# Reordering the first key matmuls of a gated linear-attention / token-MLP kernel, with smaller first copies

## The chip, the cores and the metric

The kernel runs on one core of one Trainium2 chip. The metric is the device time of an execution in microseconds (us). Executions come in a fast and in a slow state (lower granted TensorE clock); comparisons below use fast runs. A ratio is the mean time of one kernel's fast runs over the mean time of the other's of the same rounds, so it is not quite the ratio of the medians that are quoted. A profile is one execution recorded by the hardware profiler; its span runs from the first to the last instruction and is about 1.7 us shorter than the execution's time.

## The reference

Input `x` is 2048 tokens of 512 features, bf16. Two blocks are mixed by a gate per token.

```python
def _A_ref(x, wqkv, wo):                 # linear attention, 32 heads of 16
    q, k, v = ...                        # x @ wqkv, split in heads
    phi = lambda t: jnp.where(t > 0, t + 1, jnp.exp(t)) + 1e-6
    pq, pk = phi(q), phi(k)
    kv = einsum("bhsd,bhse->bhde", pk, v);  z = einsum("bhsd->bhd", pk)
    o = (pq @ kv) / (pq . z + 1e-6)
    return o @ wo
def _B_ref(x, w1, b1, w2, b2):           # MLP over tokens
    h = layernorm(x)
    u = gelu(einsum("bsd,sf->bdf", h, w1) + b1)
    return (einsum("bdf,fs->bds", u, w2) + b2).transpose
g = sigmoid((x * gate_w).sum(-1))
return g * A(x) + (1 - g) * B(x)
```

Only the first step matters here: keys `k = x @ wk` for 16 tiles of 128 tokens, followed by `phi`.

## The kernel before

The program writes the order of instructions of each engine by hand. A key matmul needs `x` transposed (features on the partitions). For most tiles a transposing DMA makes that; it is too late for the first three tiles (the first such DMA landed at 6.94 us in the profile below), so TensorE transposes those (four 128x128 matmuls with the identity), and VectorE and ScalarE copy the result from PSUM to SBUF.

```python
    # loads, in this order (x tiles are 128 KB, halves of the key weights 256 KB)
    load_x(nc.sync, 0, 1)
    load_wk(nc.scalar, 0, 2)      # chunks 0 and 1 of the key weights
    load_x(nc.sync, 1, 1)
    load_wk(nc.scalar, 2, 2)      # chunks 2 and 3
    load_x(nc.sync, 2, 1)
    # ... transposing loads of tiles 3 to 15, further weights ...
    warm_up(6)                    # six 512-column matmuls on constants

    def transpose_tile(t):
        pt = bank("pt")           # one PSUM bank of the eight
        for k in range(ND):       # ND = 4 chunks of 128 features
            mm(pt[:, k * P : (k + 1) * P], xs[:, t, k * P : (k + 1) * P], ident[:], True, True)
        H = ND // 2
        src = pt[:].rearrange("p (k s) -> p k s", k=ND)
        dst = xT[:, :, t * P : (t + 1) * P]
        nc.vector.tensor_copy(out=dst[:, 0:H], in_=src[:, 0:H])
        nc.scalar.activation(out=dst[:, H:], in_=src[:, H:], func=ACT.Copy)

    def k_part(t, ks):            # key matmuls of tile t for feature chunks ks
        if t not in kaccs:
            kaccs[t] = bank("kacc")
        for k in ks:
            mm(kaccs[t][:], xT[:, k, t * P : (t + 1) * P], wk_sb[:, k, :], k == 0, k == ND - 1)

    HEADS = 3
    transpose_tile(0)
    transpose_tile(1)
    for t in range(2):
        k_part(t, range(2))
    transpose_tile(2)
    ln_step(0)
    for t in range(HEADS):
        k_part(t, range(2 if t < 2 else 0, ND))
        k_phi(t)
    ln_step(1)
    # ... tiles 3 to 15, then queries, token MLP, outputs ...
```

## Time and profile before

| | value |
|---|---|
| time, median of 3 runs | 163.35 us (163.27 to 163.65) |
| span of the profile given | 279.7 us: this one execution fell in the slow state, granted clock 0.565 |
| TensorE busy in it | 275.8 us, 99% |
| chain of waits | 97% TensorE |

The profile's page of the kernel before: the header, the busy line of TensorE (us, share of the span, number of instructions), the granted clock in 40 slices of the span (tenths), and the chain that ended last, as shares of the span.

```profile
span 279.7 us, 2222 instructions
PE 275.8 (99%) x826; PEld 97.0 (35%) x826; DVE 128.3 (46%) x273; ACT 73.8 (26%) x114; POOL 7.2 (3%) x17
PEclk9555555555555555555555555555555555555555
PE 97%; DMA 1%; SPq 0%; DVE 0%; issue 0%
```

TensorE is the bound, by either count. What is not TensorE in the chain lies at the start, but for VectorE's last 0.35 us at the end. The timeline of TensorE there, same profile: start, duration (us), engine, line, operation, output and inputs, count, and in brackets the idle time before it with what ended it. `pt` are the transposes, `kacc` the key matmuls, `wps` the warm-up.

```profile
3.36 0.63 PE L110 MATMUL pt<-ident,xs 128*128 128x128 bf16 x4
4.28 0.61 PE L110 MATMUL pt<-ident,xs 128*128 128x128 bf16 x4 [0.29 <-DMA xs<-in_A_x_dram]
4.68 1.89 PE L110 MATMUL kacc<-wk_sb,xT 128*128 128x512 bf16 x4
6.31 0.57 PE L110 MATMUL pt<-ident,xs 128*128 128x128 bf16 x4
```

The chain of waits in order of time for the first 9 us (start, duration, what), same profile:

```profile
1.26 2.97 DMA xs<-in_A_x_dram
4.23 0.05 issue
4.28 0.61 PE pt L110 x4
4.88 1.68 PE kacc L110 x4
6.56 0.31 PE pt L110 x4
6.87 2.31 PE kacc L110 x6
```

The chain runs through the load of tile 1, which lands at 4.23 us; from there TensorE works without a hole. Tile 2 landed at 5.72 us, and its transposes stood at 6.31 us, so nobody waited for it. Up to 6.2 us the matmuls in the trace start 0.427 us apart (512 columns), half the full rate; the row PEclk does not show this. The Trainium skill, "TensorE: Matmul & The Clock Gate", Part 1, describes a cold array at half rate that rises to the full rate after some activity. This trace agrees for the first part; what follows in it is the slow state.

### The profile page before, as it was taken

The page shows a single profiled execution, that of the slowest core. Times are in us where ns is not written, and L with a number is a line of the kernel's source. Part 1 is how long each engine was busy: PE and PEld are TensorE (multiplying, and loading weights), DVE is VectorE, ACT ScalarE, POOL GpSimd, SP SyncE. Part 2 cuts the span into 40 slices and gives each one's busy share as a digit, 9 for nine tenths or more (in the row PEclk, how much of TensorE's full clock was granted, in tenths as well). Part 3 has the DMA queues.
Part 4 walks back from the last instruction along what each step waited for, and adds up shares of the span by engine and source line. Part 5 has one row for each costly group of instructions (what it writes and reads, how often), then busy time and mean ns, then how long its engine had stood idle before and what let it go on. Part 6 is the DMA issues. An engine that isn't in the chain of part 4 may idle for free.

```text
span 279.7 us, 2222 instructions
## 1 busy us (share of the span) xinstructions
PE 275.8 (99%) x826; PEld 97.0 (35%) x826; DVE 128.3 (46%) x273; ACT 73.8 (26%) x114; POOL 7.2 (3%) x17
## 2 busy tenths in 40 slices
PE   8999999999999999999999999999999999999996
PEld 3333333333333333333333333333333333333333
DVE  1835566256465571256597701565555553111111
ACT  3411344124434160235511211222222221111110
POOL 1000310010100000000000000000000000000000
PEclk9555555555555555555555555555555555555555
DMA  7999995000000008003400707000000000000000
GB/s 196 238 293 352 349 345 145 0 0 0 2 1 0 0 0 265 0 0 104 158 4 0 262 12 251 19 20 23 23 26 20 20 19 19 21 19 19 19 19 19
DMA packets 29241, 22.94 MB, mean 82 GB/s; under 512 B 7696, under 2 KB 29200, under 8 KB 29232
## 3 DMA queue, kind: packets, MB, share of 16 engines
q1 hardware_dynamic: 28288, 21.89, 26.2%
q10 hardware_dynamic: 832, 0.79, 0.8%
q0 software_dynamic: 112, 0.14, 0.2%
q8 instruction: 6, 0.10, 0.1%
q14 instruction: 3, 0.02, 0.0%
HBM read 19.01 MB, written 2.10 MB: 75 GB/s over the span
## 4 chain that ended last, share of the span: by engine, by line
PE 97%; DMA 1%; SPq 0%; DVE 0%; issue 0%
PE uacc L110 31%; PE yps L110 31%; PE kacc L110 9%; PE aps L110 9%; PE qacc L110 9%; PE gacc L110 9%; DMA xs<-in_A_x_dram 1%; PE pt L110 0%; PE kvps L110 0%; PE w2ps L110 0%; SPq L126 0%; DVE ot L500 0%; PE pt L327 0%
## 5 line engine op out<-in xcount | busy, mean ns | idle before, releaser
L110 PE MATMUL uacc<-hs,w1c 128*128 128x512 bf16 (+1 forms) x233 | 89.6, 581 | 0.0
L110 PE MATMUL yps<-uT,w2c 128*128 128x512 bf16 (+2 forms) x238 | 89.3, 560 | 0.0
L110 PEld LDWEIGHTS <-w2c 128*128 128x128 bf16 x238 | 31.2, 133 | 55.5 <-issue 55.4
L110 PEld LDWEIGHTS <-w1c 128*128 128x128 bf16 (+1 forms) x233 | 29.4, 131 | 55.3 <-issue 55.2
L500 DVE SCALAR_TENSOR_TENSOR ot<-yps,c,a_sc 128x512 bf16<-128x512 f32 (+2 forms) x17 | 12.2, 719 | 68.6 <-PE yps L110 68.6
L487 ACT ACTIVATE a_sc<-aps,c,gg 128x512 f32<-128x512 f32 x16 | 12.4, 775 | 76.0 <-PE aps L110 76.0
L110 PE MATMUL aps<-W2sb,pqT 128*128 128x512 bf16 x64 | 27.8, 582 | 0.0
L110 PE MATMUL qacc<-xT,wq_sb 128*128 128x512 bf16 x64 | 27.7, 581 | 0.0
L110 PE MATMUL kacc<-wk_sb,xT 128*128 128x512 bf16 x64 | 27.4, 589 | 0.0
L110 PE MATMUL gacc<-pk,xs 128*128 128x512 bf16 x64 | 26.8, 579 | 0.0
L211 DVE TENSOR_SCALAR e<-e 128x512 bf16<-128x512 bf16 x32 | 9.4, 293 | 34.2 <-ACT e L210 34.2
L321 ACT ACTIVATE uT<-uacc,bcol 128x512 bf16<-128x512 f32 x14 | 9.4, 686 | 46.8 <-PE uacc L110 46.8
L386 DVE STREAM_TRANSPOSE zT<-pz 128x512 f32<-128x512 f32 x16 | 11.3, 706 | 18.3 <-ACT pz L385 18.3
L210 ACT ACTIVATE e<-qacc 128x512 bf16<-128x512 f32 x16 | 9.6, 597 | 27.6 <-PE qacc L110 27.6
L210 ACT ACTIVATE e<-kacc 128x512 bf16<-128x512 f32 x16 | 9.6, 597 | 26.7 <-PE kacc L110 26.7
L110 PEld LDWEIGHTS <-xs 128*128 128x128 bf16 x76 | 9.8, 133 | 17.8 <-issue 16.3
L385 ACT ACTIVATE pz<-pqT,zcol 128x512 f32<-128x512 bf16 x16 | 11.4, 714 | 11.5 <-DVE ot L500 11.4
L110 PEld LDWEIGHTS <-wq_sb 128*128 128x128 bf16 x64 | 8.6, 135 | 16.0 <-issue 16.0
L110 PEld LDWEIGHTS <-pqT 128*128 128x128 bf16 x64 | 8.4, 132 | 16.0 <-issue 16.0
L110 PEld LDWEIGHTS <-xT 128*128 128x128 bf16 x64 | 8.2, 130 | 15.3 <-issue 14.7
L250 ACT ACTIVATE hs<-xs,nmr,rstd 128x512 bf16<-128x512 bf16 x16 | 12.7, 802 | 0.0
L395 DVE STREAM_TRANSPOSE rex<-rd 128x512 bf16<-128x512 bf16 x16 | 11.4, 711 | 0.6
(59 smaller groups left out, 116.3 us busy)
## 6 DMA issues: line engine op xcount, KB each, us to landing
w1c<-in_B_w_dram SPq DMA_DIRECT2D x7, 1024.0 KB, 12.4
w2c<-in_B_w_dram SPq DMA_DIRECT2D x8, 896.0 KB, 5.7
out_dram<-ot SPq DMA_DIRECT2D x13, 128.0 KB, 1.7
xs<-in_A_x_dram SPq DMA_DIRECT2D x3, 512.0 KB, 4.4
xs<-in_A_x_dram SPq DMA_DIRECT2D x4, 128.0 KB, 3.3
wk_sb<-in_A_wqkv_dram ACTq DMA_DIRECT2D x2, 256.0 KB, 3.3
wq_sb<-in_A_wqkv_dram SPq DMA_DIRECT2D x1, 512.0 KB, 4.8
wv_sb<-in_A_wqkv_dram SPq DMA_DIRECT2D x1, 512.0 KB, 10.0
```

The costliest lines, as they stand in the source:

```text
L110: nc.tensor.matmul(o, lhsT=lhsT, rhs=rhs, start=start, stop=stop, **kw)
L210: nc.scalar.activation(out=e[:], in_=acc[:], func=ACT.Exp)
L211: nc.vector.tensor_scalar(out=e[:], in0=e[:], scalar1=1.0, scalar2=PHI_EPS, op0=ALU.min, op1=ALU.add)
L250: nc.scalar.activation(out=hs[:, t, :], in_=xs[:, t, :], func=ACT.Identity, scale=rstd[:, t : t + 1], bias=nmr[:, t : t + 1],)
L321: nc.scalar.activation(out=uT[:, j, :], in_=acc[:], func=ACT.Gelu_apprx_tanh, bias=bcol[:, j : j + 1])
L385: nc.scalar.activation(out=pz[:], in_=seg, func=ACT.Copy, scale=zcol[:, j : j + 1])
L386: nc.vector.transpose(out=zT[:], in_=pz[:])
L395: nc.vector.transpose(out=rex[:].rearrange("p (a d) -> p a d", d=HEAD), in_=rd[:].unsqueeze(2).to_broadcast([P, SC // HEAD, HEAD]),)
L487: nc.scalar.activation(out=a_sc[:], in_=aps[:], func=ACT.Identity, scale=gg[:, t : t + 1], bias=c2[:, t : t + 1],)
L500: nc.vector.scalar_tensor_tensor(out=ot[:, :W], in0=yps[:, :W], scalar=c1[:, t : t + 1], in1=a_sc[:, cs], op0=ALU.mult, op1=ALU.add,)
```

## The change

The intent: start tile 0's key matmuls before the transposes of tiles 1 and 2, as soon as its first two chunks are copied, and make those chunks available sooner, each with its own PSUM bank and its own small VectorE copy.

```diff
+    def transpose_part(t, k0, k1, on_act):
+        pt = bank("pt")
+        for k in range(k0, k1):
+            mm(pt[:, k * P : (k + 1) * P], xs[:, t, k * P : (k + 1) * P], ident[:], True, True)
+        ...
+        if on_act:
+            nc.scalar.activation(out=dst, in_=src, func=ACT.Copy)
+        else:
+            nc.vector.tensor_copy(out=dst, in_=src)
+
     def transpose_tile(t):
-        pt = bank("pt")
-        ...                                    # one bank, VectorE half, then ScalarE half
+        transpose_part(t, 0, ND // 2, False)
+        transpose_part(t, ND // 2, ND, True)
@@
-    transpose_tile(0)
+    transpose_part(0, 0, 1, False)
+    transpose_part(0, 1, 2, False)
+    transpose_part(0, 2, ND, True)
+    k_part(0, range(2))
     transpose_tile(1)
-    for t in range(2):
-        k_part(t, range(2))
     transpose_tile(2)
+    k_part(1, range(2))
+    k_part(0, range(2, ND))
+    k_phi(0)
     ln_step(0)
-    for t in range(HEADS):
+    for t in range(1, HEADS):
         k_part(t, range(2 if t < 2 else 0, ND))
         k_phi(t)
```

TensorE's order, with T for the transposes of a tile and K for key matmuls: before T0, T1, K0(0,1), K1(0,1), T2, K0(2,3), K1(2,3), K2. After: T0, K0(0,1), T1, T2, K1(0,1), K0(2,3), K1(2,3), K2. Both issue the same twelve key matmuls, so the issue of the twelfth is a fair mark for how far the head has come.

More of the change, by code (lines that the diff above doesn't have):

```diff
@@ L196 @@
     warm_up(6)
-    def transpose_tile(t):
-        pt = bank("pt")
-        for k in range(ND):
-            mm(pt[:, k * P : (k + 1) * P], xs[:, t, k * P : (k + 1) * P], ident[:], True, True)
-        H = ND // 2
-        src = pt[:].rearrange("p (k s) -> p k s", k=ND)
-        dst = xT[:, :, t * P : (t + 1) * P]
-        nc.vector.tensor_copy(out=dst[:, 0:H], in_=src[:, 0:H])
-        nc.scalar.activation(out=dst[:, H:], in_=src[:, H:], func=ACT.Copy)
+    def transpose_part(t, k0, k1, on_act):
+        pt = bank("pt")
+        for k in range(k0, k1):
+            mm(pt[:, k * P : (k + 1) * P], xs[:, t, k * P : (k + 1) * P], ident[:], True, True)
+        src = pt[:, k0 * P : k1 * P].rearrange("p (k s) -> p k s", k=k1 - k0)
+        dst = xT[:, k0:k1, t * P : (t + 1) * P]
+        if on_act:
+            nc.scalar.activation(out=dst, in_=src, func=ACT.Copy)
+        else:
+            nc.vector.tensor_copy(out=dst, in_=src)
+    def transpose_tile(t):
+        transpose_part(t, 0, ND // 2, False)
+        transpose_part(t, ND // 2, ND, True)
     def phi(dst, acc):
```

## The prediction

> **What bounds the kernel now.** The page's busy table has TensorE busy 275.8 of 279.7 us; its chain of waits is 97% PE. That profile is in a slow state (granted clock 0.565), the timed runs are not. Estimate for the timed state: the trace has about 704 full-width (512-column) matmul slots after the head; at the warm rate in the Trainium skill, "TensorE: Matmul & The Clock Gate", Part 1 (about 215.7 ns for 512 columns; no run here shows it yet), that is about 152 us, plus 6.5 us of head, some 3 us of tail and launch is about 163. So the timed kernel too is a dense matmul stream, and only holes in the first 7 us can be won.
>
> **The head, from the timeline and the semaphore landings.** Until 6.2 us matmuls start every 0.427 us (512 columns) or 0.107 us (transposes): the half rate that the same page gives for a cold array. Landings: tile 0 at 2.98, first key-weight half 3.83, tile 1 4.23, second half 4.95, tile 2 5.72. TensorE: transposes of tile 0 start 3.36, last issued 3.68; idle 3.79 to 4.28 (tile 1's landing); tile 1's transposes; key matmuls (tile 0: 4.68, 5.11; tile 1: 5.53, 5.96) without a hole; tile 2's transposes at 6.31, by then landed for 0.6 us. From 4.28 there is no hole: the late tile 2 is hidden behind four key matmuls.
>
> **What the change does.** No matmul is added or removed. The VectorE copy of tile 0 (0.424 us for 128x256) becomes two 128x128 copies, each about 0.27 us (estimate, a line through 157 ns at 30 columns and 424 ns at 256); the first waits for one transpose instead of four: about 3.71 to 3.98. Own PSUM banks let ScalarE copy beside VectorE instead of after it (before: start 4.49, behind the VectorE copy's end at 4.45); nobody on the critical path waits for that. Tile 0's key matmuls then start near 4.1 instead of 4.68, run to about 4.95, fed by the second copy at about 4.3. Tile 1's transposes: to about 5.4. Then tile 2's transposes, now ahead of tile 1's key matmuls, need the landing at 5.72: a new hole of about 0.35 to 0.4 us. They end near 6.2; tile 1's two key matmuls follow, about 0.43 us if the clock has risen by then, 0.85 us if not.
>
> **Sum.** Estimate for the timed state, clock rising at 6.2 us in both: the same work is done at 6.53 before and about 6.63 after. The hole won (about 0.2 us net, at the half rate) is handed back as the wait for tile 2. Net +0.1 us; if tile 2 lands 0.3 us sooner in unprofiled runs, about -0.1. VectorE does the layer-norm statistics of tile 0 after phi of tile 0: its phi stream ends some 0.8 us later at tile 3, which the four-tile lag covers.
>
> **Prediction: 163.4 us, 80% range 162.9 to 164.1.** Faster by over 2%: 1%; within 2%: 98%; slower by over 2%: 1%.
>
> **What would show it.** Right: first key matmul near 4.1 to 4.2 us; a TensorE gap ending on the landing of tile 2 near 5.7; ScalarE copies no longer behind VectorE; from about 6.6 us the stream is dense, as before. Wrong: first key matmul still after 4.5 (copies or weights late); no gap before tile 2; new gaps after 7 us from VectorE's reordered queue.
>
> **What would make it wrong.** The clock: the page's gate counts activity in 3.4 us windows; if two smaller holes lower the activity enough, the warm clock comes one window later[...]; conversely earlier work could bring it sooner. Different landings without the profiler. Run-to-run spread (163.27 to 163.65) is as large as the effect.

## The result, and the profile after

The changed kernel: 163.36 us median (163.28 to 163.39, 5 runs), before 163.35 us (163.14 to 163.65, 5 runs), ratio 0.9998, 95% interval 0.9985 to 1.0012. No measurable difference. This time the profile fell in the fast state. The same lines of the changed kernel's page; it has no PEclk row.

```profile
span 161.6 us, 2223 instructions
PE 156.9 (97%) x826; PEld 71.9 (44%) x826; DVE 124.4 (77%) x274; ACT 73.1 (45%) x114; POOL 7.3 (4%) x17
PE 95%; DMA 2%; SPq 1%; DVE 0%; issue 0%
```

The share of DMA, 2% instead of 1%, says little by itself: the span is so much shorter (the kernel before, profiled in the fast state below, has 2% too). Timeline of TensorE, changed kernel:

```profile
3.35 0.48 PE L110 MATMUL pt<-ident,xs 128*128 128x128 bf16 x4
4.05 0.60 PE L110 MATMUL kacc<-wk_sb,xT 128*128 128x512 bf16 x2 [0.22 <-DMA wk_sb<-in_A_wqkv_dram]
4.50 0.39 PE L110 MATMUL pt<-ident,xs 128*128 128x128 bf16 x4
5.73 0.40 PE L110 MATMUL pt<-ident,xs 128*128 128x128 bf16 x4 [0.85 <-DMA xs<-in_A_x_dram]
5.96 1.24 PE L110 MATMUL kacc<-wk_sb,xT 128*128 128x512 bf16 x5
```

Its chain of waits in order of time:

```profile
1.73 3.96 DMA xs<-in_A_x_dram
5.68 0.05 issue
5.73 0.40 PE pt L110 x4
6.13 3.02 PE kacc L110 x14
```

The intended part happened: the first key matmuls start at 4.05 us. Two things gate them together: VectorE's first small copy ended at 3.99 us, and the first half of the key weights, the wait that the timeline names, landed at 4.01 us. So a still quicker copy could have gained nothing here. But the chain now runs through the load of tile 2, landed at 5.68 us, and TensorE stands idle 0.85 us for it.

Two things keep this pair of profiles from answering more. They are of different states. And in the changed kernel's trace the half rate ended near 3.5 us (the spacing of the transposes of tile 0 falls from 0.106 to 0.056 us), not at 6.2 us. So the kernel before was profiled again (run `a1_before_again`). Its timeline of TensorE in the fast state:

```profile
4.47 0.40 PE L110 MATMUL pt<-ident,xs 128*128 128x128 bf16 x4 [0.48 <-DMA xs<-in_A_x_dram]
4.71 1.29 PE L110 MATMUL kacc<-wk_sb,xT 128*128 128x512 bf16 x4
5.83 0.39 PE L110 MATMUL pt<-ident,xs 128*128 128x128 bf16 x4
6.05 1.24 PE L110 MATMUL kacc<-wk_sb,xT 128*128 128x512 bf16 x5
```

and its chain of waits:

```profile
1.27 3.16 DMA xs<-in_A_x_dram
4.42 0.05 issue
4.47 0.41 PE pt L110 x4
4.88 0.02 issue
4.91 0.44 DVE xT L205
5.34 0.05 issue
5.39 0.60 PE kacc L110 x2
5.99 0.22 PE pt L110 x4
6.22 2.81 PE kacc L110 x13
```

In the fast state the kernel before is bound by tile 1: landing (4.42 us), transposes, VectorE's copy (4.91 to 5.34 us), tile 1's first key matmul at 5.39 us. Tile 2 lands under that and is needed only at 5.83 us. When its transposes start, four key matmuls are done; in the changed kernel two are. That is the price of the new order: after the landing of tile 2 two more key matmuls (0.43 us at the full rate) are left to do.

### The profile page after: what moved, and what is told of

Its sections match the earlier page's. It is cut to its first block, busy times and chain, and to the rows that moved or that the text cites. A ratio compares the mean times of both kernels' runs of the same rounds, so it can differ in the third digit from the quotient of the medians.

```text
span 161.6 us, 2223 instructions
## 1 busy us (share of the span) xinstructions
PE 156.9 (97%) x826; PEld 71.9 (44%) x826; DVE 124.4 (77%) x274; ACT 73.1 (45%) x114; POOL 7.3 (4%) x17
## 4 chain that ended last, share of the span: by engine, by line
PE 95%; DMA 2%; SPq 1%; DVE 0%; issue 0%
PE uacc L110 30%; PE yps L110 30%; PE qacc L110 9%; PE gacc L110 9%; PE aps L110 9%; PE kacc L110 8%; DMA xs<-in_A_x_dram 2%; SPq L126 1%; PE kvps L110 0%; PE pt L110 0%; PE w2ps L110 0%; DVE ot L509 0%; PE pt L336 0%
## 5 line engine op out<-in xcount | busy, mean ns | idle before, releaser
L110 PE MATMUL uacc<-hs,w1c 128*128 128x512 bf16 (+1 forms) x233 | 51.5, 379 | 0.0
L110 PE MATMUL yps<-uT,w2c 128*128 128x512 bf16 (+2 forms) x238 | 51.0, 366 | 0.0
L110 PE MATMUL aps<-W2sb,pqT 128*128 128x512 bf16 x64 | 16.4, 379 | 0.0
L110 PE MATMUL qacc<-xT,wq_sb 128*128 128x512 bf16 x64 | 16.4, 379 | 0.0
L110 PE MATMUL kacc<-wk_sb,xT 128*128 128x512 bf16 x64 | 15.9, 379 | 0.2 <-DMA wk_sb<-in_A_wqkv_dram 0.2
L110 PE MATMUL gacc<-pk,xs 128*128 128x512 bf16 x64 | 15.8, 379 | 0.0
L219 DVE SCALAR_TENSOR_TENSOR pk<-kacc,e 128x512 bf16<-128x512 f32 x16 | 11.1, 692 | 0.6
L219 DVE SCALAR_TENSOR_TENSOR pqT<-qacc,e 128x512 bf16<-128x512 f32 x16 | 11.1, 692 | 0.6
L397 DVE TENSOR_REDUCE den<-zT 128x32 f32<-128x512 f32 x16 | 11.0, 686 | 0.6
L239 DVE BATCH_NORM_STATS2 stats<-xs 128x6 f32<-128x512 bf16 x16 | 10.9, 684 | 0.0
```

The lines of the kernel that those rows point to most:

```text
L110: nc.tensor.matmul(o, lhsT=lhsT, rhs=rhs, start=start, stop=stop, **kw)
L219: nc.vector.scalar_tensor_tensor(out=dst, in0=acc[:], scalar=0.0, in1=e[:], op0=ALU.max, op1=ALU.add)
L239: nc.vector.bn_stats(out=stats[:], in_=xs[:, t, :])
L397: nc.vector.tensor_reduce(out=den[:], in_=zT[:].rearrange("p (a d) -> p a d", d=HEAD), op=ALU.add, axis=AX.X)
```

## The experiments

Theory (hand-back): key matmuls are won early and given back in a wait for tile 2. Rival 1: the head does not count, a later wait absorbs any difference. Rival 2: the moment at which the half rate ends varies from run to run and hides the difference.

All twelve runs gave correct results. "Rate rises" is when the trace shows the end of the half rate: the time at which its clock record begins, which agrees with the spacing of the matmuls, or the spacing alone for the first profile of the change, which has no clock record; "12th" is the issue of the twelfth key matmul; the rest of the profile's columns are of that same execution. Times are medians over all runs.

| run | rate rises | tile 1, tile 2 landed | 12th | span | time | before, same chip |
|---|---|---|---|---|---|---|
| first profile of the change | 3.5 | 4.36, 5.68 | 7.905 | 161.605 | 163.36 | 163.35 |
| a1_before_again | 4.28 | 4.42, 5.65 | 7.564 | 161.271 | 163.01 | 163.15 |
| a2_tile2_late | 3.97 | 4.85, 5.83 | 7.876 | 161.576 | 163.34 | 163.15 |
| a3_copies_only | 4.56 | 4.34, 5.75 | 7.542 | 161.245 | 163.12 | 163.15 |
| a4_order_only | 6.26 | 4.30, 5.76 | 8.440 | 162.136 | 163.84 | 163.15 |
| b0_after_again | 5.09 | 4.29, 5.66 | 7.883 | 161.584 | 163.55 | 163.10 |
| b1_load2_early | 6.33 | 4.27, 5.13 | 8.005 | 161.713 | 163.34 | 163.10 |
| b3_fill3 | 4.87 | 4.44, 5.62 | 7.936 | 161.634 | 163.52 | 163.10 |
| b4_fill8 | 3.86 | 4.41, 5.82 | 8.631 | 162.331 | 164.96 | 163.10 |
| c2_tile2_late_again | 4.79 | 4.48, 5.96 | 7.854 | 161.550 | 163.37 | 163.13 |
| c3_after_third | 5.97 | 4.21, 5.75 | 8.036 | 161.747 | 163.46 | 163.13 |
| c1_tiles_first | 4.29 | 3.52, 4.19 | 7.603 | 161.311 | 163.35 | 163.13 |
| c4_tiles_first_banks | 5.02 | 3.42, 5.04 | 7.895 | 161.594 | 163.28 | 163.13 |

Span minus 12th is 153.70 us in all thirteen, from 153.696 to 153.711. So everything after the head takes the same time, whatever the head does. The time of the same execution minus the 12th is nearly constant as well (155.40 to 155.46 us), so the time of a run without a profile also tells about when its twelfth key matmul was issued.

### a1_before_again: the kernel before, unchanged

> The kernel before, unchanged, for a profile in the fast state and as a null. Theory (hand-back): in the changed kernel's fast profile TensorE leaves the half rate at 3.5 us, not at 6.2 us, and waits 0.85 us for tile 2. With the same early rise the kernel before should wait about 0.35 us for the copy of tile 1 (near 5.05 to 5.40 us), none for tile 2, and issue its twelfth key matmul near 7.56 us, 0.35 us before the changed kernel's 7.905 us; span about 161.3 us, time about 163.0. Rival 1 (the head does not count, a later wait absorbs it): span 161.6 us whatever the head. Rival 2 (the rise of the clock varies from run to run): a rise near 6.2 us, twelfth key matmul near 8.0 us, time about 163.5. Ratio as a null: 1.000 within 0.0015.

Measured: 12th at 7.564 us, span 161.271 us, 163.01 us. These are the numbers expected for an early rise, and rival 1 falls: the span follows the head. The null ratio is 0.9973 (0.9936 to 1.001), off by more than the stated 0.0015. One of the eleven other runs of the kernel before took 165.04 us and counts as fast; it widens every ratio of this set (the a runs). The medians, 163.01 and 163.15 for the same code, show how far a difference of 0.14 us can be trusted.

### a2_tile2_late and c2_tile2_late_again: tile 2 behind tile 1's key matmuls

```diff
-    transpose_tile(2)
     k_part(1, range(2))
+    transpose_tile(2)
```

> The change with one part undone: tile 2's transposes stand behind tile 1's two key matmuls again. Theory: the 0.85 us wait for tile 2 shrinks to under 0.1 us, a wait of about 0.55 us for the copy of tile 1 takes part of its place (4.72 to 5.28 us), the twelfth key matmul issues near 7.45 us instead of 7.905 us, the time falls to about 162.9 us with an early rise of the clock, ratio about 0.997 to 0.998. Rival 1: head earlier, span unchanged at 161.6 us, ratio 1.000. With a late rise (6.2 us): about 163.6 us.

> The kernel with tile 2 behind tile 1's key matmuls (single-chunk copies kept), run again, since in its first profile tile 1 landed at 4.85 us instead of 4.2 to 4.4 us and hid the effect. Hand-back theory, with tile 1 landed by 4.4 us and the half rate ended by 4.3 us: tile 1's first key matmul near 5.3 us, no wait of tile 2's transposes, twelfth key matmul near 7.45 us, time about 162.9 us. With the half rate ending near 6.2 us: about 8.1 us and 163.55 us. If instead this order also costs what the changed one does, with an early end: 7.9 us and 163.35 us.

Measured: the first profile had tile 1 landing late (4.85 us), so it told little; the repeat had it at 4.48 us. The wait for tile 2 is gone in both, but the 12th key matmul came at 7.854 us, not 7.45 us, and the medians are 163.34 and 163.37 us, hardly better than the changed kernel (163.46 us beside the repeat). One of the six runs of `a2_tile2_late` was slow (165.36 us). In the repeat the half rate lasted until 4.79 us, later than the expectation's condition. The chain of waits of `c2_tile2_late_again` shows what that does:

```profile
4.16 0.89 PE kacc L110 x2
5.05 0.13 PE pt L110 x2
5.17 0.02 issue
5.20 0.44 DVE xT L207
5.63 0.05 issue
5.68 0.60 PE kacc L110 x2
```

Tile 0's two key matmuls, ahead of tile 1's transposes and mostly at half rate, push those to 4.88 us although tile 1 had landed at 4.48 us; the copy follows at 5.20 to 5.62 us, tile 1's first key matmul at 5.68 us. In the kernel before (a1) tile 1's transposes go in at once (4.47 us) and the key matmuls of tile 0 cover most of the copy: TensorE could have issued the next one at 5.14 us and issues it at 5.39 us. So there is a second gate, close beside tile 2's landing: tile 1's copy, late in this profile because the half rate lasted into tile 0's key matmuls. Two of the twelve runs of this order took 162.88 us, the value expected for an early rise; the others took 163.29 us or more. That the rate rose early in these two is not shown; they have no profile.

### a3_copies_only: small copies and separate banks in the old order

```diff
     # order of the kernel before, with transpose_part as in the change
-    transpose_tile(0)
+    transpose_part(0, 0, 1, False)
+    transpose_part(0, 1, 2, False)
+    transpose_part(0, 2, ND, True)
     transpose_tile(1)
     for t in range(2):
         k_part(t, range(2))
     transpose_tile(2)
```

> The other half alone: single-chunk VectorE copies of tile 0 and separate PSUM banks for the two copies of each tile, in the order of the kernel before. Theory: the first key matmul stays behind tile 1's landing and transposes (about 4.65 us), but tile 1's copy no longer waits for tile 0's, so its key matmul starts near 5.25 us; no wait for tile 2; twelfth key matmul near 7.5 us with an early rise; time about 162.95 us. Rival 1: 163.35 us as all.

Measured: tile 1's first key matmul at 5.25 us, 12th at 7.542 us, as expected; 163.12 us against 163.15 us. The first key matmul is at 4.68 us, behind tile 1's transposes. The copies alone neither help nor hurt measurably.

### a4_order_only: the new order with the old copies

```diff
     # order of the changed kernel; transpose_tile as in the kernel before
+    transpose_tile(0)
-    transpose_part(0, 0, 1, False)
-    transpose_part(0, 1, 2, False)
-    transpose_part(0, 2, ND, True)
     k_part(0, range(2))
     transpose_tile(1)
     transpose_tile(2)
```

> The new order alone, with the old copies (one bank, one 256-column VectorE copy, ScalarE behind it). Theory: the first key matmul starts about 0.3 us later than in the changed kernel (near 4.35 us), and this costs nothing, because tile 2's landing near 5.7 us still gates: twelfth key matmul at 7.9 us, time 163.35 us, the same as the changed kernel. If the copies mattered: about 0.3 us slower than the changed kernel, 163.65 us.

Measured: a miss. Five of six runs took 163.84 to 163.88 us, one 163.38 us, the value expected. In the profiled run the half rate lasted until 6.26 us, and there the copies do gate. Its chain of waits:

```profile
4.02 0.44 DVE xT L205
4.46 0.05 issue
4.51 1.03 PE kacc L110 x2
5.54 0.44 PE pt L110 x4
5.98 0.02 issue
6.00 0.44 DVE xT L205
6.44 0.05 issue
6.49 2.55 PE kacc L110 x11
```

No load is in this stretch. TensorE and VectorE take turns: copy of tile 0, its key matmuls, transposes of tile 1, copy of tile 1. The 12th key matmul, at 8.440 us, is 0.40 us later than in the changed kernel's profile with the rise nearest to this one (c3: 5.97 us, 12th at 8.036 us). The rise is 0.29 us later here, which at half the rate can be at most about 0.15 us of that (an estimate); the rest falls to the old copies. In times the ratio to the kernel before is 1.0019 (0.9985 to 1.0054), an interval that holds 1 because of the 165.04 us run; still, five of the six runs are slower than ten of the eleven of the kernel before. So the order alone probably makes the head slower than before, and the small copies buy part of that back; this is how the two halves of the change belong together.

### b0_after_again and c3_after_third: the changed kernel again

> The changed kernel again, on one chip with runs of the kernel before. So far five profiles give span minus start of the twelfth key matmul = 153.70 us within 0.01 us, so the head passes to the time one for one; and the half rate of TensorE ended at 3.5, 4.0, 4.3, 4.9 and 6.3 us in them. Hand-back theory with an early end of the half rate (before 4.5 us): twelfth key matmul at 7.9 us, time about 163.35, against 163.0 of the kernel before: ratio about 1.002. With a late end (6.2 us): 8.15 us and 163.6, against 163.5. Rival (the change gains or costs nothing even with an early end): ratio 1.000 and twelfth key matmul at 7.56 us.

> The changed kernel once more on one chip with the kernel before, to settle the size: the two comparisons so far gave ratios 0.9998 and 1.0018. Hand-back theory: ratio between 1.0005 and 1.0025, that is 0.1 to 0.4 us slower, by how often the half rate ends early; wait for tile 2 present in the profile unless the half rate ends after 5.5 us. Rival (no difference at all): 0.9995 to 1.0005.

Measured: 163.55 us against 163.10 us, ratio 1.0018 (0.9999 to 1.0038); 163.46 us against 163.13 us, ratio 1.0010 (0.9998 to 1.0022). (The 4.9 us in the first expectation was a misreading: the rate rose at 4.56 us in a3.) With the first comparison (0.9998) the three average 1.0009, about 0.15 us. Each interval holds 1, so the size, and strictly even the sign, is not settled by times. In the profiles the 12th key matmul stands at 7.883 us (rise 5.09 us) and 8.036 us (5.97 us), against 7.564 us in the one fast profile of the kernel before (rise 4.28 us). Both wait for tile 2 again, but only 0.33 and 0.28 us: when the half rate lasts longer, TensorE's own work fills the rest. The lines of tile 2's transposes in the timelines of TensorE, `b0_after_again` first, then `c3_after_third`:

```profile
5.71 0.40 PE L110 MATMUL pt<-ident,xs 128*128 128x128 bf16 x4 [0.33 <-DMA xs<-in_A_x_dram]
5.79 0.47 PE L110 MATMUL pt<-ident,xs 128*128 128x128 bf16 x4 [0.28 <-DMA xs<-in_A_x_dram]
```

No fast profile of the kernel before has a late rise. An estimate can be made from its slow profile, which ran its head at half rate until 6.22 us: with the full rate from tile 2's transposes (6.31 us) on, the 12th would be issued near 8.04 us. The changed kernel, its c3 profile carried to the same rise, comes to about 8.15 us. So the loss would be some 0.3 us with an early rise and about 0.1 us with a late one; the second figure is not shown by a run. Nor was it tested whether the order itself moves the rise.

### b1_load2_early: tile 2 loaded ahead of the second half of the key weights

```diff
     load_x(nc.sync, 1, 1)
-    load_wk(nc.scalar, 2, 2)
     load_x(nc.sync, 2, 1)
+    load_wk(nc.sync, 2, 2)
```

> The changed kernel with tile 2 loaded ahead of the second half of the key weights. If tile 2's landing is what gates the changed order: tile 2 lands near 4.7 us instead of 5.7 us, the wait of 0.85 us before its transposes goes, tile 1's key matmul starts near 5.3 us (its copy gates), tile 0's third key matmul near 5.7 us, the twelfth near 7.2 us, time about 162.7 us with an early end of the half rate, ratio about 0.996. If the landing did not gate: 7.9 us and 163.35 us as before.

Measured: tile 2 landed at 5.13 us and nobody waited for it: between 3 and 9 us the table of waits has no entry for TensorE at all. But the gain was small: 163.34 us against 163.55 us of the changed kernel in the same set, 0.2 us instead of 0.65 us, and the 12th key matmul at 8.005 us in a profile whose half rate lasted to 6.33 us (c3: 8.036 us at 5.97 us). The order of work in this trace is seamless but for the copy of tile 1, 5.34 to 5.77 us, after which tile 1's key matmul starts at 5.82 us. Taking away the wait for tile 2 thus uncovers TensorE's half-rate work and tile 1's copy. The theory as stated, tile 2 as the one gate, is too simple. What this kernel does with an early rise, the case of the expectation, no profile shows; none of its six runs came below 163.20 us.

### b3_fill3 and b4_fill8: extra matmuls in the hole

```diff
     transpose_tile(1)
+    warm_up(3)        # b4_fill8: warm_up(8); 512 columns each, result unused
     transpose_tile(2)
```

> The changed kernel with three further 512-column warm-up matmuls (result unused) between the transposes of tile 1 and of tile 2. If TensorE only waits there for tile 2 (hole of 1.01 us between issues), 3 x 0.216 = 0.65 us of work fit in and cost nothing: twelfth key matmul at 7.9 us, time 163.35 us with an early end of the half rate. If the head were bound by TensorE work: 0.65 us more, 164.0 us. With a late end of the half rate (6.2 us) they are 1.28 us and cost about 0.9 us.

> The same with eight such matmuls, 1.73 us at the full rate, 0.72 us more than the hole. Hand-back theory: twelfth key matmul near 8.6 us, span about 162.3 us, time about 164.1 us with an early end of the half rate; the wait for tile 2 is gone. Rival (a later wait absorbs the head): 163.35 us still.

Measured: three further matmuls cost nothing, 163.52 us against 163.55 us of the changed kernel in the same set, 12th at 7.936 us. The timeline of TensorE of `b3_fill3` shows them between the transposes of tile 1 and 2:

```profile
4.89 0.39 PE L110 MATMUL pt<-ident,xs 128*128 128x128 bf16 x4
5.12 0.82 PE L110 MATMUL wps<-const-bfloat16-1.0 128*128 128x512 bf16 x3
5.77 0.38 PE L110 MATMUL pt<-ident,xs 128*128 128x128 bf16 x4
```

Eight cost: 12th at 8.631 us in the profiled run (rise 3.86 us), 164.04 us there, as expected; but the median is 164.96 us and the slowest run 165.26 us, which eight matmuls at half rate (3.4 us instead of 1.7 us) in other runs would account for; no profile of such a run exists. So TensorE had room for at least 0.6 us of work at this place in the run of `b3_fill3` (rise 4.87 us), and for about 1.0 us with an early rise: eight matmuls, 1.75 us, issued the 12th 0.73 us later than in the first profile of the change (7.905 us, rise 3.5 us). What goes beyond the room is paid at the end. This too speaks against rival 1.

### c1_tiles_first and c4_tiles_first_banks: all three tiles loaded sooner

```diff
     load_x(nc.sync, 0, 1)
-    load_wk(nc.scalar, 0, 2)
-    load_x(nc.sync, 1, 1)
-    load_wk(nc.scalar, 2, 2)
-    load_x(nc.sync, 2, 1)
+    load_x(nc.scalar, 1, 1)
+    load_wk(nc.sync, 0, 2)
+    load_x(nc.scalar, 2, 1)
+    load_wk(nc.sync, 2, 2)
```

The rest is the kernel before; the second of the two also has two banks for each tile.

> The kernel before with only its first loads reordered: tiles 0 and 1 first, then the first half of the key weights, tile 2, the second half. If the head is bound by what lands when, the stream becomes dense at about 4.5 us instead of 5.4 us: first key matmul near 4.5 us, twelfth near 7.15 us against 7.56 us with an early end of the half rate, time about 162.6 us against 163.0 us; with a late end (6.2 us) about 163.4 us against 163.5 us. Ratio about 0.998. If landings do not bound: ratio 1.000.

> The same reordered loads with the changed kernel's two PSUM banks for each tile's transposes (whole-tile order as in the kernel before), so that VectorE and ScalarE copy at the same time: key matmuls from about 4.35 us, twelfth near 7.0 us with an early end of the half rate, time about 162.5 us, 0.1 us below the run without the banks; ratio to before about 0.997.

Measured: both miss. 163.35 us (ratio 1.0014, 1.0000 to 1.0028) and 163.28 us (ratio 1.0025, 0.9994 to 1.0056), against 163.13 us. All tiles were there early, but now the first half of the key weights landed at 4.97 and 5.26 us, against about 4.0 us in the other runs, and the key matmuls wait for it. The waits of TensorE in `c4_tiles_first_banks` after 3 us (engine, line, waited for, us in total, times, longest):

```profile
PE kacc L110 <- DMA wk_sb<-in_A_wqkv_dram: 0.9, 1, 0.9
```

Tile 2, issued on the other queue at about the same time, landed before those weights in both. The Trainium skill, "DMA: Bandwidth & Descriptors", section "Issuing engines are not separate DMA queues", says that transfers from several engines run on the same 16 DMA engines and interleave; these landings agree. Everything the head needs is 896 KB (three tiles and both halves of the key weights) through one pipe, the last of it landed near 5.7 us in the old order, and in both of these runs, what one piece gained in being put first another lost. No version measurably beat the kernel before.

## Why the prediction was right, point by point

- **Time**: 163.4 us predicted, 163.36 us measured, inside the range; "within 2%" was right. The figure was easy to hit: it is the measured 163.35 us plus 0.1 us, in a range 1.2 us wide. The mechanism was right in the points below; that the wrong moment of the rise did no harm to the figure was luck.
- **What bounds the kernel**: right, and stronger than argued. The rest of the execution after the twelfth key matmul is 153.70 us in thirteen profiles, within 0.015 us.
- **The small copies**: predicted about 0.27 us each and a first key matmul "near 4.1"; measured 0.292 and 0.280 us, and 4.05 us. The two engines did copy side by side (VectorE from 3.70 us, ScalarE from 3.87 us). The Trainium skill, "PSUM — Partial Sum Buffer", section "PSUM bank collisions raise a hardware error", says that two engines may not access one bank (in one partition quadrant) at once; this agrees with the kernel before, where ScalarE began 0.03 us after VectorE had ended, in all three tiles.
- **The new hole before tile 2**: right in place and cause; predicted 0.35 to 0.4 us, measured 0.85, 0.33 and 0.28 us in three profiles. The large value belongs to the early rise of the clock.
- **"clock rising at 6.2 us in both"**: wrong. The rate rose anywhere between 3.5 and 6.3 us in the fast profiles. The 6.2 us had been read from one profile. The term of the sum that this touches is "Net +0.1 us": in the profiles the head of the changed kernel, for rises at 3.5 and 5.1 us, is 0.34 and 0.32 us later than the one fast profile of the kernel before (rise at 4.28 us, so not the same). For the rise at 6.2 us that the prediction assumed, the estimate under b0 gives about +0.1 us, as predicted. In times it averages 0.15 us, which is not distinguishable from zero.
- **"The hole won ... is handed back as the wait for tile 2"**: half of the story. Removing that wait, by the order (c2) or by the load (b1), brought at most 0.2 us in the medians; in both of their profiles the half rate lasted into tile 0's key matmuls, and tile 1's copy stood right behind the wait. The new order delays tile 1's transposes behind two key matmuls and leaves the copy of tile 1 to be covered by what follows; the kernel before hid most of it behind tile 0's key matmuls.
- **"the four-tile lag covers" VectorE's later work**: right; no new hole after 7 us.

Of the rivals, the first falls. The second is half right: the rise does vary and does blur the times, but the wait for tile 2 and the later twelfth key matmul are there in all three profiles of the changed kernel, set against a single fast profile of the kernel before.

What stays open: the exact size of the difference in times (0.15 us, with intervals that hold zero), and what the runs of the kernel before near 163.7 us look like, since its only fast profile was of a 162.97 us run. That a late rise makes them is not shown, and it may not be the whole of it: by the constant of 155.4 us, 163.7 us means a twelfth key matmul near 8.3 us, later than the estimate of 8.04 us for a late rise.

## What to carry to other kernels

At the start of a kernel every operand arrives at its own time, so write down the landings first: an early start of one matmul is worth something only if the matmuls left over still cover the next landing and the next copy. Matmuls that are ready are cover; spending them early uncovers a latency later. And before trusting a difference of a few tenths of a microsecond in the head, profile both kernels in the same state more than once: here the end of TensorE's half rate moved by 2.8 us between executions.

## What the Trainium skill lacked or had wrong

- "TensorE: Matmul & The Clock Gate", Part 1: it puts the transition at around 4 us into sustained matmul activity, plus or minus 0.5 us. Here, with the first matmul at 0.84 us and holes in the activity after it, it came 2.7 to 5.5 us later (3.5 to 6.3 us), a far wider spread. The same Part also warns that the number of slow matmuls varies from run to run (6, 11 or 14 for one kernel), which fits better; a reader should not rely on the 0.5 us. Its spacings agree: 0.427 us for 512 columns before, 0.216 us after.
- No page says that the granted clock of a profile leaves this half rate out: the page of the kernel before gives tenths of 9 in the first slice, while matmuls ran at half rate until 6.2 us. Their spacing shows it, and so does the time at which the trace's clock record begins (6.22 us there, 4.28 us in a1); the row counts the time before that as full.
- "VectorE: DVE Perf Modes", the cycle table of the TRN2 errata section: 120 cycles plus one per column for PSUM to SBUF gives, at its 0.96 GHz, about 0.39 us for 256 columns and 0.26 us for 128 (estimates from that page); measured 0.424 us and 0.280 to 0.292 us.
